# Attention decode with a gMLP branch: load order of x, the third chunk of the last output product, and the shape of two weight pieces

## The chip, the cores and the metric

The kernel runs on one core of a Trainium2 chip. The metric is the device time of one execution in microseconds. A profiled execution also leaves a trace, whose clock starts with the span; all points in time below are microseconds from there.

## The reference

Everything is bf16; B = 4 sequences, one new token each, D = 640.

```python
xn = layernorm(x)
# A: attention over a cache. 32 heads, 4096 keys, head size 128
q = (xn @ wq)                                   # wq: 640 x 4096
p = softmax(q . k_cache * 128**-0.5)            # k_cache, v_cache: 4 x 32 x 4096 x 128
a = (p . v_cache) @ wo                          # wo: 4096 x 640
# B: gated MLP
z = gelu(xn @ w_in)                             # w_in: 640 x 1728, halves z1 and z2
g = w_sp * layernorm(z2) + b_sp                 # w_sp and b_sp are scalars here (one token)
out = x + a + (z1 * g) @ w_out                  # w_out: 864 x 640
```

The two caches are 268 MB of the 282 MB that are read.

## The kernel before

**Loads.** SP's queue carries nearly all bytes, in an order written out in the code: wq (L126), w_in (L129), the first 256 rows of w_out (L132), three pieces of the rest of w_out (`load_piece`, L138), then K and V by units (`load_unit`, L192) and wo (`load_wo`, L200). A unit is 8 heads of one sequence, 8 MB; there are 16 of K and 16 of V. They share five slots of the tile `kv`, so a unit's load waits until what stood in its slot has been read. ACT's queue carries x (L120) and the scalars w_sp and b_sp (L122, L123); POOL's carries two more pieces of w_out (L138) and two small dummy transfers (`step`, L145), which turn POOL's choice of transfer engine so that the pieces fall on chosen ones.

The table `PC` (L62) describes the five pieces: first and last partition, first column chunk, chunks n, and how the rows of w_out are dealt (k, run). Each row of `PC` is one DMA of (last - first) partitions with n / run runs each. The same table drives the z matmuls (L349) and the gelu copies (L363, L366), so that z's columns stand where the rows of w_out do. The pieces land in `w_words`, whose memory the transposed K words take later.

DMAs of SP and ACT take eight completion semaphores in turn, in the order in which the tile framework has placed them; a DMA waits until the one that held its semaphore before has landed. The order before is: w_sp, wq, b_sp, x, w_in, w_out, piece 0, piece 1, piece 2, K unit 0. So piece 2, the ninth, waits for w_sp, and K unit 0 for wq.

**Start.** x waits for a memset on POOL (L118). It goes through a layer norm (L216 to L229) into `xnT` (L233), then q (L304) and z (L342, L349); z runs through gelu, its own layer norm and the gate (L355 to L396), and is multiplied with w_out into `proj` (L409), which frees `w_words`.

**K and V.** DVE transposes K as 32-bit words (L431), PE forms scores (L442); per group of 32 (head, sequence) pairs follow the softmax and the probabilities in `Zb` (L475 to L479). PE multiplies them with V into `O` (L513), and `emit_sel` and `emit_oT` reduce the result to `oT`.

**Tail.** `o_mul` (L556) multiplies a chunk of `oT` with a chunk of wo. The chunks of groups 0 to 2 are summed in `proj`, on partitions 0 to 31 and 32 to 63 by turns, where x (L294) and the gMLP (L409) have been added too. wo of the last group comes in four parts, cut at chunks 4, 6 and 7. Its chunks 0 to 2 still go to `proj`, 320 columns at a time (L604); `o_1` (L608) and `o_q` (L612) then add the two halves of `proj`. Chunks 3 to 7 go to `last`, 160 columns at a time, on two groups of partitions. `o_bf` (L623) adds `last` and `o_q`, and SP and ACT write one half each.

Of the kernel before, what the change touches and what calls it, by code (L numbers as in the profile page):

```python
# [16 lines left out]
def kernel(  # L17
# [19 lines left out]
    nc = tc.nc  # L37
    P = 128
    B, Sq, D = A_x.shape
# [3 lines left out]
    HG = 8  # L43
# [8 lines left out]
    NG = H // HG  # L52
# [6 lines left out]
    nf = FA * P  # L59


    PC = ((0, 20, 0, 10, 5, 10), (32, 44, 0, 11, 3, 11), (0, 4, 10, 3, 3, 1), (60, 68, 0, 24, 2, 24), (92, 96, 0, 18, 3, 6))  # L62
    f_at = [nf]
    for p0, p1, _, n, _, _ in PC:
        f_at.append(f_at[-1] + (p1 - p0) * n)
# [3 lines left out]
    NH = 2  # L69
    NO2 = NOUT // NH  # L70
# [35 lines left out]
    def at_slot(i, n, off=0):  # L106
        return kv[:, i * SL + off:i * SL + off + n]


    x_flat = A_x.rearrange("b s d -> (b s) d")  # L110
# [5 lines left out]
    ln_t = at_slot(0, 8 * D, n_q)  # L116
    XR = 2 * B
    nc.gpsimd.memset(ln_t[:32, :].bitcast(F32).rearrange("p (a n) -> p a n", a=8)[:, 0::7, :], 0.0)  # L118
    x_bf = ln_t[:XR, 0:D]
    nc.scalar.dma_start(out=ln_t[1:XR:2, 0:D], in_=x_flat)  # L120
    sb_bf = const.tile([1, 2], BF16)
    nc.scalar.dma_start(out=sb_bf[:, 0:1], in_=B_w_sp)  # L122
    nc.scalar.dma_start(out=sb_bf[:, 1:2], in_=B_b_sp[None, :])  # L123

    wq = at_slot(0, n_q).rearrange("p (c n) -> p c n", c=DC)
    nc.sync.dma_start(out=wq, in_=A_wq.rearrange("(p c) n -> p c n", c=DC))  # L126
# [9 lines left out]
    def load_piece(eng, t):  # L136
        p0, p1, c0, n, k, run = PC[t]
        return eng.dma_start(out=w_rest[p0:p1, c0:c0 + n].rearrange("p c n -> p (c n)"),  # L138
                             in_=B_w_out[f_at[t]:f_at[t + 1], :].rearrange("(r i c) n -> i r (c n)", i=k, c=run))
# [135 lines left out]
    for q in range(4):  # L275
        nc.gpsimd.tensor_copy(out=SelE[32 * q:32 * q + 32, :, q % 2, :],
                              in_=b8[32 * q:32 * q + 32, 8:8 + HP, None].to_broadcast((32, HP, P // HG)))
# [10 lines left out]
                          in_=ident_f[:].rearrange("p (q x c) -> p q x c", q=2, c=C2))  # L288


    proj = ps_j.tile([64, 512], F32)
# [8 lines left out]
    for hf in range(2):  # L300
        for c in range(DC):
            for j in range(NG):
                n0 = j * HG * Dh + hf * 512
# [21 lines left out]
    z_in = [[], [], [], []]  # L325
    for t, (p0, p1, _, n, k, run) in enumerate(PC):
        src = w_z[:, :, :, f_at[t]:f_at[t + 1]]
        for q in range(p0 // 32, (p1 - 1) // 32 + 1):
            x0, x1 = max(p0, 32 * q), min(p1, 32 * q + 32)
            if x1 - x0 == p1 - p0 and run == n:  # L330
                cols = [src]
            elif run == 1:
                cols = [src.rearrange("p d a (r i) -> p d a i r", i=k)]
            else:
                i_r = src.rearrange("p d a (r i c) -> p d i a r c", i=k, c=run)
                cols = [i_r[:, :, i] for i in range((x0 - p0) * k // (p1 - p0), (x1 - p0) * k // (p1 - p0))]
            z_in[q].append((t, x0 - 32 * q, x1 - 32 * q, cols))
    z_of = [[sum((x1 - x0) * PC[t][3] for t, x0, x1, _ in z[:m]) for m in range(len(z) + 1)] for z in z_in]
    w_za = w_z[:, :, :, 0:nf].rearrange("p c a (q j i) -> p c q a i j", q=4, j=32)
    for c in range(DC):  # L340
        for q in range(4):
            nc.tensor.matmul(z_ps[32 * q:32 * q + 32], lhsT=xnT[:, c, :], rhs=w_za[:, c, q], start=(c == 0), stop=(c == DC - 1))  # L342
        for q in range(4):
            parts = []
            for m, (t, x0, x1, cols) in enumerate(z_in[q]):
                f = (x1 - x0) * PC[t][3] // len(cols)
                parts += [(z_of[q][m] + f * i, f, src) for i, src in enumerate(cols)]
# [8 lines left out]
    for q in range(4):  # L356
        rows = slice(32 * q, 32 * q + 32)
        for m, (t, x0, x1, _) in enumerate(z_in[q]):
            p0, p1, c0, n, k, run = PC[t]
            z = zr_ps[rows, :, z_of[q][m]:z_of[q][m + 1]]  # L360
# [3 lines left out]
            else:  # L364
                for a in range(2):
                    nc.scalar.activation(out=dst[:, a].rearrange("p c (i r) -> p c i r", i=k),  # L366
                                         in_=z[:, a].rearrange("p (r i c) -> p c i r", i=k, c=n), func=ACT.Gelu_apprx_tanh)
# [184 lines left out]
    def o_mul(dst, g, c, hf, n0, n1, start, stop):  # L552

        nb = 32 if start else RW
        c0 = RW * c + 1 - hf
        nc.tensor.matmul(dst[0:nb, 0:n1 - n0], lhsT=state[("oT", g)][:, c0:c0 + nb], rhs=wo_t[g][:, c, n0:n1],  # L556
                         start=start, stop=stop)
# [43 lines left out]
    emit_oT(NG - 1)  # L601
    emit_proj(NG - 2, (1,))

    for c, hf in ((0, 0), (1, 0), (0, 1), (1, 1), (2, 0), (2, 1)):  # L604
        p = min(c, 1)
        o_mul(proj[32 * p:32 * p + 32], NG - 1, c, hf, hf * NO2, (hf + 1) * NO2, False, (c, hf) in ((0, 1), (2, 1)))
    o_1 = ppool.tile([32, NO2], F32, tag="p", name="o_1")
    nc.vector.tensor_copy(out=o_1[:], in_=proj[0:32, 0:NO2])  # L608
    NQ = NO2 // 2
# [2 lines left out]
        nc.vector.tensor_tensor(out=o_q[32 * k:32 * k + 32, :], in0=proj[32:64, k * NQ:(k + 1) * NQ],  # L612
                                in1=o_1[:, k * NQ:(k + 1) * NQ], op=ALU.add)
    last = ps_l.tile([64, NQ], F32)
    for c in range(3, HG):
        for hf in range(NH):
            for k in range(2):
                n0 = hf * NO2 + k * NQ
                o_mul(last[32 * k:32 * k + 32], NG - 1, c, hf, n0, n0 + NQ, c == 3 and hf == 0,
                      c == HG - 1 and hf == NH - 1)  # L620

    o_bf = ppool.tile([64, NQ], BF16, tag="p", name="o_bf")
# [32 lines left out]
```

## Time and profile before

| what | value |
|---|---|
| three runs | 663.15, 663.48, 663.49 us; median 663.48 |
| profiled execution | 663.49 us; span in its trace 661.7 us |
| busy share of the span | DVE 57%, PE 43%, ACT 11%, POOL 11% |
| read from HBM | 282.26 MB, 427 GB/s over the span |
| first load issued | 0.72 us |
| x issued on ACT, its first reader starts | 1.57, 10.94 us |
| first K unit issued | 17.58 us |
| last DVE operation (L623), output issued | 658.89, 659.24 us |

The page's slices cut the span into 40 parts of 16.5 us with each engine's busy share in tenths. The chain of waits goes back from the last instruction, at each step to what released it. In the timeline a row has start, duration, engine, line and operation, and in brackets how long the engine was idle before it and which work ended that. The trace also records single packets of the transfer engines (queue, start, time, size) and the moments at which semaphores count up; a DMA counts up once for each transfer engine that carries a share of it, as that share lands.

### The profile page before, as it was taken

Reading aid. Unit: us, or ns where it says so; the run is one execution under the profiler, and the core shown is the slowest. Engines: PE = TensorE matmul, PEld = TensorE weight load, DVE = VectorE, ACT = ScalarE, POOL = GpSimd, SP = SyncE. Lnnn points to the kernel's source line nnn. Section 1 sums busy time; section 2 is a strip of 40 time slices with the busy share of each in tenths; the row PEclk is TensorE's granted clock in tenths of the full one; section 3 lists DMA queues with packets and bytes.
Section 4 is the critical chain, followed back from the end, with each engine's and each line's share of the span. In section 5 each row is a group of like instructions: output and inputs, shape, how many; then the busy total and the mean of one; then the engine's idle time right before and its main releaser. Section 6 shows DMA issues by size and latency. Waiting matters only on the chain.

```text
span 661.7 us, 5539 instructions
## 1 busy us (share of the span) xinstructions
PE 284.1 (43%) x2303; PEld 108.1 (16%) x2303; DVE 379.7 (57%) x307; ACT 74.1 (11%) x145; POOL 74.2 (11%) x140
## 2 busy tenths in 40 slices
PE   0445555446062356335325065532606254641246
PEld 0221111112021121111102022110202112220012
DVE  6339989766191758718356196764619175971112
ACT  0310000240100000330200000070100000042200
POOL 4540000030200000130300000030110000002300
PEclk9998778679677686766959587765858759666768
DMA  8999999999999999999999999999999999999997
GB/s 367 474 413 428 425 440 445 440 421 428 417 444 441 440 405 436 441 441 440 421 440 412 441 426 439 440 433 424 437 432 440 433 428 415 454 424 437 422 418 288
DMA packets 7241, 282.61 MB, mean 427 GB/s; under 512 B 1120, under 2 KB 1405, under 8 KB 1801
## 3 DMA queue, kind: packets, MB, share of 16 engines
q1 hardware_dynamic: 6837, 281.91, 98.8%
q8 instruction: 18, 0.29, 0.2%
q0 software_dynamic: 352, 0.35, 0.2%
q14 instruction: 6, 0.05, 0.0%
q10 hardware_dynamic: 28, 0.01, 0.0%
HBM read 282.26 MB, written 0.01 MB: 427 GB/s over the span
## 4 chain that ended last, share of the span: by engine, by line
DMA 71%; DVE 12%; issue 11%; PE 2%; POOL 1%; ACT 1%; SPq 0%; DVEq 0%; POOLq 0%; ACTq 0%
DMA kv<-in_A_k_cache_dram 59%; DVE w_words L431 11%; DMA kv<-in_A_v_cache_dram 5%; DMA kv<-in_B_w_in_dram 4%; DMA kv<-in_A_wo_dram 4%; PE O L513 1%; POOL kv L393 0%; PE proj L409 0%; DVE w_words L493 0%; DVE w_words L475 0%; POOL z_b L395 0%; POOL kv L378 0%; ACT L355 0%; DVE m L449 0%; ACT w_words L487 0%
## 5 line engine op out<-in xcount | busy, mean ns | idle before, releaser
L431 DVE STREAM_TRANSPOSE w_words<-kv 128x2048 f32<-128x2048 f32 x128 | 282.8, 2275 | 121.3 <-DMA kv<-in_A_k_cache_dram 118.7
L442 PE MATMUL S<-w_words,QZ 128*32 128x512 bf16 x1024 | 182.7, 488 | 256.1 <-DVE w_words L431 256.1
L442 PEld LDWEIGHTS <-QZ 128*32 128x32 bf16 x1024 | 58.8, 109 | 377.8 <-issue 313.6
L513 PE MATMUL O<-kv,w_words 128*32 128x512 bf16 x1024 | 73.2, 449 | 57.9 <-DMA kv<-in_A_v_cache_dram 50.8
L479 ACT ACTIVATE w_words<-w_words,MkE 32x128 bf16<-32x128 bf16 x120 | 60.9, 507 | 115.8 <-PE O L513 102.7
L522 DVE TENSOR_TENSOR om<-O,Mk 128x512 f32<-128x512 f32 x15 | 10.4, 692 | 94.1 <-PE O L513 94.1
L477 POOL TENSOR_SCALAR w_words<-w_words,MkE 32x128 bf16<-32x128 bf16 x60 | 43.4, 723 | 137.3 <-PE O L513 108.4
L513 PEld LDWEIGHTS <-w_words 128*32 128x32 bf16 x1024 | 33.5, 110 | 96.9 <-issue 67.6
L487 ACT ACTIVATE w_words<-S,negmax 128x1024 bf16<-128x1024 f32 x4 | 4.5, 1114 | 400.1 <-DVE negmax L459 311.7
L475 DVE TENSOR_SCALAR w_words<-w_words,MkE 32x128 bf16<-32x128 bf16 x76 | 24.6, 324 | 2.3
L417 POOL COPY QZ<-qT 32x32 bf16<-32x32 bf16 x16 | 5.1, 318 | 173.0 <-PE S L442 172.5
L523 DVE TENSOR_REDUCE R<-om 128x128 f32<-128x512 f32 x15 | 15.3, 1020 | 0.5
L498 POOL TENSOR_SCALAR rs<-MkB,rowsum 128x4 f32<-128x4 f32 x4 | 1.2, 299 | 112.7 <-ACT w_words L487 112.7
L493 DVE STREAM_TRANSPOSE w_words<-w_words 128x1024 bf16<-128x1024 bf16 (+1 forms) x8 | 9.6, 1241 | 5.6 <-ACT w_words L487 5.6
L546 POOL MEMSET oT<- 128x66 bf16 x4 | 0.5, 156 | 97.5 <-PE proj L556 97.5
L449 DVE TENSOR_REDUCE m<-S 128x1 f32<-128x1024 f32 x4 | 4.9, 1225 | 6.1 <-PE S L442 6.1
L133 DVE MEMSET w_words<- 128x7680 f32 x1 | 6.5, 6458 | 2.4 <-issue 2.4
L535 PE MATMUL misc<-R,SelX 128*128 128x512 f32 x8 | 4.5, 645 | 7.2 <-DVE R L523 5.5
L525 DVE TENSOR_SCALAR R<-O,Mk 128x128 f32<-128x128 f32 x1 | 0.4, 351 | 12.5 <-PE O L513 12.5
L304 PE MATMUL q<-kv,xnT 128*32 128x512 bf16 x40 | 4.5, 631 | 6.5 <-DVE xnT L233 6.5
L500 PE MATMUL misc<-rs,SelE 128*128 128x4 f32 x8 | 2.3, 364 | 10.4 <-POOL rs L498 10.4
L556 PE MATMUL proj<-kv,oT 128*8 128x320 bf16 x54 | 5.2, 333 | 1.6 <-DMA kv<-in_A_wo_dram 1.6
(105 smaller groups left out, 95.1 us busy)
## 6 DMA issues: line engine op xcount, KB each, us to landing
kv<-in_A_k_cache_dram SPq DMA_DIRECT2D x8, 4096.0 KB, 30.1
kv<-in_A_v_cache_dram SPq DMA_DIRECT2D x1, 6144.0 KB
kv<-in_A_wq_dram SPq DMA_DIRECT2D x1, 5120.0 KB, 16.8
kv<-in_A_wo_dram SPq DMA_DIRECT2D x3, 1280.0 KB
kv<-in_B_w_in_dram SPq DMA_DIRECT2D x1, 2160.0 KB, 23.9
kv<-in_A_v_cache_dram SPq DMA_DIRECT2D x1, 2048.0 KB
kv<-in_A_wo_dram SPq DMA_DIRECT2D x1, 640.0 KB, 23.6
kv<-in_B_w_out_dram SPq DMA_DIRECT2D x1, 320.0 KB
```

The costliest lines, as they stand in the source:

```text
L133: nc.vector.memset(w_words[:, 0:FR * NOUT // 2], 0.0)
L417: nc.gpsimd.tensor_copy(out=QZ[r0:r0 + 32, :, :, :, 8 + 8 * hp], in_=qT[32 * g:32 * g + 32, NE * hp:NE * hp + NE].rearrange("p e a b -> p ...
L431: nc.vector.transpose(kT.rearrange("p (t r) -> p t r", r=32), kw)
L442: nc.tensor.matmul(S_ps[32 * q:32 * q + 32, i], lhsT=QZ[:, b, 2 * kh + w, e, w0:w0 + 32], rhs=kb[:, i, :, e, :, w], start=(b == 0 and k < ...
L475: nc.vector.tensor_scalar(out=dst, in0=src, scalar1=mk, scalar2=None, op0=ALU.mult)
L477: nc.gpsimd.tensor_scalar(out=dst, in0=src, scalar1=mk, scalar2=None, op0=ALU.mult)
L479: nc.scalar.activation(out=dst, in_=src, func=ACT.Copy, scale=mk)
L493: nc.vector.transpose(pT_t[:, j0:j1, :], blocks)
L513: nc.tensor.matmul(O_ps[32 * q:32 * q + 32, :, :], lhsT=Zb[b % 2][:, w].rearrange("p h c -> p (h c)"), rhs=vv[:, w * 4 * Dh:(w + 1) * 4 * ...
L522: nc.vector.tensor_tensor(out=om4[:], in0=O_ps[:], in1=Mk4[:, :, None].to_broadcast((P, 4, Dh)), op=ALU.mult)
L523: nc.vector.tensor_reduce(out=R, in_=om4[:].rearrange("p c d -> p d c"), axis=AX.X, op=ALU.add)
L556: nc.tensor.matmul(dst[0:nb, 0:n1 - n0], lhsT=state[("oT", g)][:, c0:c0 + nb], rhs=wo_t[g][:, c, n0:n1], start=start, stop=stop)
```

## The change

It has three parts. x is loaded as two DMAs of two rows each on ACT's queue, and the two scalars are held back until the second of them has been issued. Two pieces of w_out, piece 2 on SP and piece 4 on POOL, go on three partitions instead of four, with the same number of rows and half as many runs; the special case of a run of one goes. In the tail, chunk 2 of the last group moves from `proj` to `last`. Since the number of DMAs ahead of the K loads grows by one and x now comes behind wq in the count, the waits on the eight semaphores move too: the order is wq, x part one, x part two, w_sp, b_sp, w_in, w_out, piece 0, piece 1, piece 2, K unit 0.

```diff
-    PC = ((0, 20, 0, 10, 5, 10), (32, 44, 0, 11, 3, 11), (0, 4, 10, 3, 3, 1), (60, 68, 0, 24, 2, 24), (92, 96, 0, 18, 3, 6))
+    PC = ((0, 20, 0, 10, 5, 10), (32, 44, 0, 11, 3, 11), (0, 3, 10, 4, 2, 2), (60, 68, 0, 24, 2, 24), (92, 95, 0, 24, 2, 12))
...
-    nc.scalar.dma_start(out=ln_t[1:XR:2, 0:D], in_=x_flat)
+    for b0 in range(0, B, 2):
+        x_in = nc.scalar.dma_start(out=ln_t[1 + 2 * b0:5 + 2 * b0:2, 0:D], in_=x_flat[b0:b0 + 2, :])
     sb_bf = const.tile([1, 2], BF16)
-    nc.scalar.dma_start(out=sb_bf[:, 0:1], in_=B_w_sp)
-    nc.scalar.dma_start(out=sb_bf[:, 1:2], in_=B_b_sp[None, :])
+    with tc.issue_after(x_in.ins):
+        nc.scalar.dma_start(out=sb_bf[:, 0:1], in_=B_w_sp)
+        nc.scalar.dma_start(out=sb_bf[:, 1:2], in_=B_b_sp[None, :])
...
-            elif run == 1:
-                cols = [src.rearrange("p d a (r i) -> p d a i r", i=k)]
...
-    for c, hf in ((0, 0), (1, 0), (0, 1), (1, 1), (2, 0), (2, 1)):
-        p = min(c, 1)
-        o_mul(proj[32 * p:32 * p + 32], NG - 1, c, hf, hf * NO2, (hf + 1) * NO2, False, (c, hf) in ((0, 1), (2, 1)))
+    for c, hf in ((0, 0), (1, 0), (0, 1), (1, 1)):
+        o_mul(proj[32 * c:32 * c + 32], NG - 1, c, hf, hf * NO2, (hf + 1) * NO2, False, hf == NH - 1)
...
-    for c in range(3, HG):
+    for c in range(2, HG):
         for hf in range(NH):
             for k in range(2):
                 n0 = hf * NO2 + k * NQ
-                o_mul(last[32 * k:32 * k + 32], NG - 1, c, hf, n0, n0 + NQ, c == 3 and hf == 0,
+                o_mul(last[32 * k:32 * k + 32], NG - 1, c, hf, n0, n0 + NQ, c == 2 and hf == 0,
                       c == HG - 1 and hf == NH - 1)
```

## The prediction

> **What bounds the kernel now.** I read the page first: the slices (part 2), the queues (part 3) and the chain (part 4).
>
> ```profile
> span 661.7 us, 5539 instructions
> DMA  8999999999999999999999999999999999999997
> q1 hardware_dynamic: 6837, 281.91, 98.8%
> q8 instruction: 18, 0.29, 0.2%
> DMA 71%; DVE 12%; issue 11%; PE 2%; POOL 1%; ACT 1%; SPq 0%; DVEq 0%; POOLq 0%; ACTq 0%
> ```
>
> The transfer engines are busy from the first slice to the last: queue 1, which SP feeds, alone takes 98.8% of sixteen engines' span. The chain's "DMA 71%" understates this; its DVE and issue parts lie beside running transfers, since each load is issued while earlier ones are still queued. The load of K unit 2 shows how far ahead: issued at 54.88, while the engine that is first through K unit 1 lands its part only at 59.84 (semaphore records of the trace). So a delay in the first 50 us costs nothing unless it leaves an engine's ring empty.
>
> Next the chain of waits over the last 22 us.
>
> ```profile
> 633.20 23.64 DMA kv<-in_A_wo_dram
> 656.84 0.04 issue
> 656.88 0.44 PE proj L556 x4
> 657.32 0.06 PE last L556
> 657.38 0.22 PE proj L556 x2
> 657.60 0.02 issue
> 657.63 0.49 DVE o L608
> 658.12 0.02 issue
> 658.14 0.32 DVE o_q L612
> 658.46 0.01 issue
> 658.47 0.33 DVE o_q L612
> 658.80 0.03 issue
> 658.83 0.02 DVEq L623
> 658.85 0.04 issue
> 658.89 0.32 DVE o_bf L623
> ```
>
> It names DVE as last before `o_bf`, but by a hair: PE's last matmul into `last` ends at 658.76, as the last piece of wo lands at 658.41.
>
> Third, the timeline of the start.
>
> ```profile
> 1.57 0.68 ACTq L120 DMA_DIRECT2D kv<-in_A_x_dram  x1
> 8.88 2.49 SPq L138 DMA_DIRECT2D w_words<-in_B_w_out_dram  x3
> 18.16 4.46 PE L304 MATMUL q<-kv,xnT 128*32 128x512 bf16 x40 [6.54 <-DVE xnT L233]
> 25.08 0.30 PE L342 MATMUL misc<-kv,xnT 128*32 128x128 bf16 x4 [2.46 <-DMA kv<-in_B_w_in_dram]
> ```
>
> x feeds the layer norm, then q; but what PE waits for next, 2.46 us long, is w_in, not x.
>
> **The tail.** Two 320-column matmuls of chunk 2 leave `proj`; four of 160 columns join `last`. `proj` is then complete with the group of four that ends at 657.32 (individual records: 657.32 for the last of them) rather than at 657.59, so `o_1` and both `o_q` move 0.27 us forward and end at about 658.53. Now PE is last: its end at 658.76 stays, since the four matmuls of chunk 7 start only when that chunk has landed (658.41), and PE has gaps ahead of chunks 4, 6 and 7. From PE's end to DVE's start took 0.04 us at L608 (657.59 to 657.63). So `o_bf` starts at 658.80 instead of 658.89: **-0.10 us**, all that this edit can give; 0.17 of the 0.27 us meet the wait for the last piece. The extra two matmuls (about 0.07 us each at the pitch of `last`, 1.33 us for 18) lie in the gap before chunk 4, which lands at 657.61. Were that cover gone they would cost up to 0.14 us.
>
> **x ahead, in two parts.** Before, the semaphore records show three rows of x landing at 8.94 to 9.19 and the fourth at 10.90, on the engine that had carried both scalars, the second of which landed at 7.83. On that engine packets of ACT's queue take turns with packets of wq: the second scalar's word at 5.83, its semaphore at 7.39, the row of x at 8.91, each one wq packet (1.51 us) apart. After, part one waits for POOL's memset (ends 1.34) and is issued at about 1.4, part two at about 2.0. Each engine used carries a row and a semaphore, and where both parts use the same engines that twice over: four turns, the first at 5.8 to 7.0, the last 4.54 us later, plus 0.5 to land: 10.8 to 12.0. If the parts went to different engines, 8.9 to 9.2. I take the first, since two scalars from ACT shared one engine.
> The Trainium skill (DMA: Bandwidth & Descriptors, the section on why a DMA increments its semaphore by 16) says that a DMA runs on the lowest-numbered k engines, k dividing the slowest dimensions. By that both parts sit on engines 0 and 1, which speaks against the split; the trace agrees, with x and the scalars meeting on one engine.
> Either way it costs nothing: q would end at 22.62 + 1.1 = 23.7 at the latest, before w_in lands at 25.04. Beyond that, z's chain has 4.96 us of queued loads as cover (59.84 - 54.88). The scalars, now behind x, land before 20 and are used at 29.03.
>
> **Pieces on three partitions.** The same rows in half as many descriptors. SP's piece 2: 12 packets of 1,280 B at 0.055 us become 6 of 2,560 B at 0.102: 0.66 to 0.61 us on its one engine. POOL's piece 4: 12 of 7,680 B at 0.291 (3.49 us) become 6 of 15,360 B, between 0.291 and 0.615 (16,384 B) and near the latter; by interpolation 0.575, 3.45 us. PE's z matmuls stay at 40 of L349 and ACT's gelu at the same elements. The engine that got x's fourth row carries one more row of x (+0.055). All this is under 0.1 us on single engines, and none is the last one: at the landing of 658.41 the last engine trails the next by 0.15 us, and it became last in one step of 1.5 us at 634.9, where the 17th instruction packet (16,384 B on queue 8, 1.10 us) fell on it. Effect 0 (between -0.04 and +0.06).
>
> **The moved waits.** Of the DMAs of SP and ACT each takes the next of eight semaphores and waits until its last holder has landed. One more DMA, and x behind wq in the count, shift the holders. Piece 1 now waits for wq (17.56) where it waited for nothing; piece 2 for part one of x; K unit 0, which waited for wq, for part two of x. Queued behind piece 1 on SP are piece 2 and K unit 0, and K unit 0's issue moves from 17.58 to 17.58 + 0.75 + 0.69 (the issues of pieces 1 and 2) + 0.09 = 19.11. Eight engines have no pieces of queue 1; the packet records show seven of them reaching K unit 0 at 20.73 to 20.98 and the eighth at 21.37. From issue to first packet there is one row with empty rings, wq: issued 0.72, first packets 1.75 to 2.77, that is 1.03 to 2.05 later. Counted until it streams at full rate (first packet of 1.51 us done at 3.97 to 4.88) it is 1.74 to 2.65. So K unit 0 can start at 20.14 to 21.16, or stream from 20.85 to 21.76. Seven engines may lose 0 to 1.03 us, the eighth 0 to 0.39. The eighth, by its distance to the others, is the one that ends last (2.9 us ahead at 45.55, and last after two steps of 1.5 us, each at an instruction packet), so it counts in full. The other seven have cover: 0.31 us for one of them, which the 18th fetch hits, and 1.8 or more for the rest. A gain is excluded, since a later issue brings nothing forward. Cost: **0 to +0.72 us** (1.03 - 0.31); I take +0.1, since wq's start was cold and here all queues run.
> The Trainium skill (the same page, on latency) gives 0.6 us to a first byte from SP's queue; by that the rings would never run dry and the term is 0. Wq's row of 1.03 and more differs, and I go by the row.
>
> **Sum.** The profiled execution took 663.49 us, 1.79 more than its span, and stands 0.01 over the median of the three runs (663.48). 663.49 - 0.10 (tail) + 0 (x) + 0 (pieces) + 0.1 (K unit 0) = **663.5**. A measurement of this kernel tells some 0.2% (1.3 us) from no change.
>
> **Rivals.**
> *The ring runs dry (slower).* K unit 0 comes so late that the last engine stalls. For it: 1.53 us later on SP, with 1.6 us from the new issue to the first empty ring. Against: the last engine has 2.26 us (21.37 - 19.11), and only its loss counts. Each microsecond after that is one at the end, so it is over 0.2% from 3.7 us between issue and stream (2.26 + 1.33 + 0.10), 1.0 more than wq's worst. It would give about 665.0. A late part two of x does the same, from 17.56 + 1.5 = 19.1 on. Chance 0.14.
> *The engines end more evenly (faster).* At 658.41 the sixteen engines lead the last one by 0 to 2.48 us, 1.09 on average. Perfect balance would give 663.49 - 1.09 - 0.10 = 662.3, still within 0.2%, but nothing here moves bytes between the last engine and the others. Over 0.2% needs more than balance: 0.04.
> *x is on the path (faster or not as said).* If x set the start, part one at 9.0 instead of 10.9 would give -1.9 us, 661.6. Against it stands the 2.46 us wait for w_in. Chance 0.01.
> *The main case*, all covers hold: 0.81, with 663.39 to 664.1 by the bounds above.
>
> **Numbers.** Median noise adds 0.3 us on either side. The range from 662.8 to 664.9 leaves out the dry ring's long end and the small gains. Faster by over 0.2% 0.05, within 0.2% 0.81, slower 0.14.
>
> **What would show it.** In the profile after: `o_bf` waits for PE's `last`, not `o_q`, and starts some 0.04 us after PE's end; the first K issue of L194 on SP stands near 19.1 with pieces 1 and 2 between 17.6 and 19.1; slices of DMA still 9; PE's wait before the z matmuls still ends on w_in near 25. Wrong would be: a DMA slice of 8 near 20 us, last wo landing later than 658.9 or earlier than 658, or z's matmuls waiting for q or x.

## The result and the profile after

The changed kernel takes 664.37 us (median of 22 runs, 664.00 to 664.71) against 663.35 for the kernel before on the same chip (22 runs, 663.15 to 663.53): +1.02 us, a ratio of 1.0016 [1.0009, 1.0022]. That is a small, real loss, just inside the 0.2% that the prediction set as the bound of no change, and 0.9 us above its number. The profiled execution took 664.16 us, with a span of 662.2.

The page after: span, slices (busy share of the transfer engines in tenths, and GB/s, per 1/40 of the span) and chain.

```profile
span 662.2 us, 5547 instructions
...
DMA  9999999999999999999999999999999999999997
GB/s 369 435 428 431 425 424 452 435 428 431 433 439 432 443 399 449 440 440 431 409 435 432 439 420 444 431 432 424 441 439 443 428 428 413 435 440 443 421 412 290
...
DMA 74%; issue 10%; DVE 9%; PE 4%; POOL 1%; ACT 1%; SPq 0%; DVEq 0%; POOLq 0%; ACTq 0%
```

And the GB/s line of the page of before, which the prediction had not shown:

```profile
GB/s 367 474 413 428 425 440 445 440 421 428 417 444 441 440 405 436 441 441 440 421 440 412 441 426 439 440 433 424 437 432 440 433 428 415 454 424 437 422 418 288
```

The busy line says 9 from end to end, but the second slice (16.6 to 33.1 us) shows 435 GB/s where it showed 474. The line counts a packet whole in the slice in which it starts, which makes the fall look larger than it is: with each packet spread over its own time, the slice moves 408 GB/s where it moved 429. By the packet records, spread in this way, 34.27 MB had moved by 82.7 us after the change and 34.59 before; at 427 GB/s the 0.32 MB are 0.75 us, and the gap is there by 30 us (11.45 and 11.79 MB). Some 0.25 us of it are engines without a packet (the time in packets between 20 and 25 us, averaged over the sixteen engines, falls from 5.07 to 4.83 us; the records overlap a little); the rest are packets that take longer. A longer packet counts as busy, and 0.25 us is little in a slice of 16.5, so the sign that the prediction named (a busy slice of 8) could not show this.

The timeline of SP, and then of PE, at the start:

```profile
8.88 10.36 SPq L140 DMA_DIRECT2D w_words<-in_B_w_out_dram  x3
19.28 0.38 SPq L194 DMA_DIRECT2D kv<-in_A_k_cache_dram  x1
```

```profile
19.26 3.88 PE L306 MATMUL q<-kv,xnT 128*32 128x512 bf16 x40 [6.34 <-DVE xnT L235]
25.56 0.24 PE L342 MATMUL misc<-kv,xnT 128*32 128x128 bf16 x4 [2.42 <-DMA kv<-in_B_w_in_dram]
```

The three pieces, which took SP's queue 2.49 us, now stretch over 10.36: piece 1 is issued at 17.77, piece 2 at 18.56 (the single instructions in the trace), K unit 0 at 19.28 instead of 17.58. q starts 1.1 us later and z's matmuls still wait for w_in (landed at 25.52, before at 25.04), so x is not on the path.

The chain at the end:

```profile
634.96 24.17 DMA kv<-in_A_wo_dram
659.13 0.04 issue
659.17 0.32 PE last L556 x4
659.49 0.02 issue
659.51 0.32 DVE o_bf L622
```

PE is now last before `o_bf`, as the tail edit intends (`o_q` had ended at 659.24). But the last piece of wo lands at 659.13, and landed at 658.41 before: +0.72 us, and all that follows comes that much later, less the 0.10 of the tail (`o_bf` 659.51 against 658.89).

### The profile page after: what moved, and what is told of

Read it like the earlier page. It is cut to its first block, busy times and chain, and to the rows that moved or that the text cites. A ratio compares the mean times of both kernels' runs of the same rounds, so it can differ in the third digit from the quotient of the medians.

```text
span 662.2 us, 5547 instructions
## 1 busy us (share of the span) xinstructions
PE 290.1 (44%) x2305; PEld 109.1 (16%) x2305; DVE 379.6 (57%) x307; ACT 74.1 (11%) x145; POOL 73.0 (11%) x140
## 4 chain that ended last, share of the span: by engine, by line
DMA 74%; issue 10%; DVE 9%; PE 4%; POOL 1%; ACT 1%; SPq 0%; DVEq 0%; POOLq 0%; ACTq 0%
DMA kv<-in_A_k_cache_dram 46%; DMA kv<-in_A_v_cache_dram 21%; DVE w_words L431 9%; DMA kv<-in_B_w_in_dram 4%; DMA kv<-in_A_wo_dram 4%; PE O L513 3%; POOL kv L393 0%; PE proj L409 0%; POOL z_b L395 0%; PE S L442 0%; SPq L202 0%; POOL kv L378 0%; ACT L355 0%; PE misc L342 0%; DVE z_b L396 0%
## 5 line engine op out<-in xcount | busy, mean ns | idle before, releaser
L442 PE MATMUL S<-w_words,QZ 128*32 128x512 bf16 x1024 | 188.5, 501 | 252.2 <-DVE w_words L431 252.2
L513 PE MATMUL O<-kv,w_words 128*32 128x512 bf16 x1024 | 75.6, 460 | 56.0 <-DMA kv<-in_A_v_cache_dram 52.8
```

Source lines behind the costliest of these rows:

```text
L442: nc.tensor.matmul(S_ps[32 * q:32 * q + 32, i], lhsT=QZ[:, b, 2 * kh + w, e, w0:w0 + 32], rhs=kb[:, i, :, e, :, w], start=(b == 0 and k < ...
L513: nc.tensor.matmul(O_ps[32 * q:32 * q + 32, :, :], lhsT=Zb[b % 2][:, w].rearrange("p h c -> p (h c)"), rhs=vv[:, w * 4 * Dh:(w + 1) * 4 * ...
```

## The experiments

A transfer engine works through what is queued for it, its ring; the ring runs dry when the engine has finished that before the next load arrives.

**Theory:** K unit 0 is issued too late to reach the transfer engines before eight of them run out of queued work. The transfer engines have no idle time later in which to make that up, so the loss stays to the end. **Rivals:** the pieces or the tail cost it; the two parts of x cost it; more DMAs cost it as such; the pieces issued late right in front of K unit 0 do.

All results first. "First packets" are the first 64 KB packets of K unit 0 on the eight engines without pieces: the range of their starts and of the time each took. An undisturbed one takes 2.42 us; one that takes longer is called stretched. "Moved" is what all packets had carried by 82.7 us. The change of the median is against the kernel before on the same chip.

| kernel | K unit 0 issued | first packets start | took | moved, MB | last wo landed | median |
|---|---|---|---|---|---|---|
| before | 17.58 | 20.73–21.37 | 2.42 | 34.59 | 658.41 | |
| x one part, scalars late (e9) | 11.40 | 20.37–21.02 | 2.42 | 34.61 | 658.20 | +0.01 |
| pieces only (e2) | 17.72 | 20.54–21.03 | 2.42 | 34.64 | 658.01 | +0.06 |
| tail only (e3) | 17.78 | 20.52–21.05 | 2.42 | 34.60 | 658.20 | -0.06 |
| scalars late (e4) | 17.80 | 20.44–21.02 | 2.42–2.48 | 34.62 | 658.09 | +0.12 |
| K unit 0 behind a DVE copy (e10) | 17.82 | 20.61–21.10 | 2.42–2.47 | 34.62 | 658.20 | +0.04 |
| x one part (e7) | 18.34 | 20.63–22.42 | 2.78–4.13 | 34.28 | 659.51 | +1.30 |
| one spare load (e5) | 18.41 | 20.86–22.08 | 2.64–3.79 | 34.24 | 659.71 | +1.29 |
| K unit 0 behind DVE transposes (e12) | 18.78 | 20.92–21.73 | 2.81–3.72 | 34.22 | 660.07 | +1.39 |
| two spare loads (e6) | 19.18 | 20.87–21.68 | 2.83–3.46 | 34.27 | 659.08 | +1.46 |
| x part only (e1) | 19.24 | 20.74–22.04 | 2.51–3.72 | 34.24 | 659.14 | +1.37 |
| **the change** | 19.28 | 20.80–21.87 | 2.74–3.57 | 34.27 | 659.13 | +1.02 |
| K unit 0 behind a POOL copy (e11) | 19.54 | 21.13–22.14 | 2.53–3.56 | 34.22 | 659.36 | +1.26 |
| three spare loads (e8) | 20.16 | 21.50–22.67 | 2.62–3.89 | 34.06 | 660.02 | +2.31 |

**The three parts, one at a time.** The kernel before with the x part alone, the new `PC` alone, and the new tail alone (the diffs are those of the change).

> Only the x part of the change on the kernel before: two parts of x ahead of the scalars, so that the waits move as in the whole change. Theory (K unit 0 issued 1.7 us later, rings of eight transfer engines run empty near 20.8 us): first K issue at 19.2 to 19.4, last piece of wo lands 0.5 to 0.8 us later than before, time +0.9 to +1.2 us. Rival A (the new piece shapes slow single engines): 0. Rival B (later x delays the z chain): also slower, but then PE's wait before the z matmuls no longer ends on w_in.

> Only the three-partition pieces. Theory: within 0.15 us of before, first K issue at 17.6. Rival A: +0.7 to +1.0 us.

> Only chunk 2 moved to last. Theory: -0.10 us, PE's last ends the wait of o_bf, which starts 0.02 to 0.05 us after PE's end. A rival in which the two extra matmuls are in the way: 0 to +0.14 us.

x alone: 664.57 against 663.20, 1.0020 [1.0012, 1.0029]. Pieces alone: 663.26, 1.0001 [0.9992, 1.0010]. Tail alone: 663.14, 0.9999 [0.9991, 1.0008]. The loss sits in the x part. At +1.37 us that part alone costs more than I had expected (+0.9 to +1.2), and 0.35 more than the whole change; no run takes this difference apart. The tail's 0.1 us is smaller than the runs can resolve; its mechanism shows in the chain of the tail alone, where PE takes DVE's place and `o_bf` follows it at once:

```profile
658.20 0.04 issue
658.25 0.32 PE last L556 x4
658.57 0.02 issue
658.59 0.32 DVE o_bf L622
```

**x's two parts or K unit 0.** The whole change, with the scalars issued later still, behind the activation of rstd. x keeps its two parts and lands as late, but K unit 0 again waits for wq, as before, and no piece waits.

```diff
-    with tc.issue_after(x_in.ins):
-        nc.scalar.dma_start(out=sb_bf[:, 0:1], in_=B_w_sp)
-        nc.scalar.dma_start(out=sb_bf[:, 1:2], in_=B_b_sp[None, :])
...
+    act = nc.scalar.activation(out=rstd[:], ...)
+    with tc.issue_after(act.ins):
+        (the two scalars)
```

> The whole change, but the two scalars are loaded after the first square root on ACT, behind K unit 0 in the count of semaphores: piece 1 and piece 2 wait for nothing, K unit 0 waits for wq as before. x stays in two parts and lands as late as in the change. Theory: first K issue back at 17.6, no stretched first packets, time -0.1 us against before (663.25). Rival A or B: still +0.9 to +1.1 us.

663.32 against 663.20, 1.0002 [0.9993, 1.0011]: the loss is gone. SP's timeline and the GB/s line of this run:

```profile
8.88 2.48 SPq L137 DMA_DIRECT2D w_words<-in_B_w_out_dram  x3
17.80 0.36 SPq L191 DMA_DIRECT2D kv<-in_A_k_cache_dram  x1
```

```profile
GB/s 370 471 413 428 425 439 447 436 421 424 430 440 441 440 403 438 441 441 432 429 424 428 441 418 443 440 425 436 438 432 428 429 436 419 446 436 422 423 425 296
```

The pieces are back in one group, K unit 0 is 1.48 us earlier, and the second slice is 471 again. x in two parts costs nothing, nor do more DMAs as such, since this run has as many as the change; where they stand in the count of semaphores does.

**The same with x in one part.** K unit 0 then is eighth and waits for no semaphore.

> The whole change, but x in one DMA ahead of the scalars, and the scalars behind the first square root on ACT: now K unit 0 is the eighth DMA in the count and waits for nothing, so it is issued at about 11.4 instead of 17.6. Theory: no ring was empty before, so this gains nothing over the version with late scalars; with the tail's 0.1 us 663.1 to 663.3. Rival (even at 17.6 the issue of K unit 0 costs something): 662.8 or less.

Issued at 11.40, six microseconds earlier than before, for 663.26 against 663.25, 1.0000 [0.9991, 1.0009]. Earlier than needed brings nothing.

**Spare loads: a dose of lateness.** The kernel before with one, two or three more loads of w_sp on ACT into a scratch tile, which shift the semaphores like the change does.

```diff
+    spare = const.tile([1, 2], BF16)     # [1, 4] for three
+    for i in range(1):     # 2, 3
+        nc.scalar.dma_start(out=spare[:, i:i + 1], in_=B_w_sp)
```

> The kernel before with one more DMA on ACT behind x: a second load of the scalar w_sp into a spare tile that nobody reads. It moves the count of semaphores by one: piece 2 waits for wq, K unit 0 is issued behind it. Nothing else of the change is in it. Theory: K unit 0 issued at 18.4 to 18.5; with the 2.6 us from issue to full rate that the change showed it streams from 21.1, where the first rings end at 20.5 to 20.9: 0.2 to 0.6 us lost on the early engines, most of it covered at the end; time +0.1 to +0.4 us. Rival (x's place or its two parts, not the waits, made the change slow): 0.

> The kernel before with two such spare loads on ACT: pieces 1 and 2 and K unit 0 are all issued behind wq, as in the change; x, pieces and tail as before. Theory: K unit 0 issued at 19.2, time +1.0 to +1.4 us, as the x part alone gave. Rival: 0.

> Three such spare loads: piece 0 waits for wq as well, so K unit 0 is issued at about 20.2, one microsecond later than with two. Theory: rings empty from 20.5 on for all engines, each further microsecond of delay is one at the end: +1.8 to +2.4 us. Rival (a fixed loss for any gap): as with two.

One: 664.54 against 663.25, 1.0020 [1.0011, 1.0029]. Two: 664.71, 1.0022 [1.0013, 1.0031], at +1.46 just above what I had expected. Three: 665.56, 1.0034 [1.0022, 1.0047]. Here my expectation of one load failed: I had it at +0.1 to +0.4 by adding a fixed delay to the issue, and it cost as much as two. So the medians make no ramp: nothing up to 17.82, then at once 1.3, flat to 19.3, and 2.3 at 20.16. With three loads, though, piece 0 is late too (17.64 instead of 8.88), so that last step is not K unit 0's lateness alone. And single runs spread at the edge: with one load ten of eleven runs lie between 664.48 and 664.94, and one at 663.56.

**x in one part, whole change otherwise.** Fewer DMAs, K unit 0 half as late.

```diff
-    for b0 in range(0, B, 2):
-        x_in = nc.scalar.dma_start(out=ln_t[1 + 2 * b0:5 + 2 * b0:2, 0:D], in_=x_flat[b0:b0 + 2, :])
+    x_in = nc.scalar.dma_start(out=ln_t[1:XR:2, 0:D], in_=x_flat)
```

> The whole change, but x in one DMA, still ahead of the two scalars. As many DMAs as before; x in the first place shifts the completion semaphores, so piece 2 waits for wq near 17.6 us and K unit 0 queues behind it, issued near 18.4 us instead of 19.28. The tail and the pieces on three partitions stay. Theory one (any issue later than about 17.8 us empties the rings): +0.9 to +1.4 us, 664.1 to 664.6. Rival (the second part of x is what costs): 0 to +0.2 us, 663.2 to 663.4.

664.55 against 663.25, 1.0018 [1.0009, 1.0026]. The second part of x is not what costs. Its eleven runs spread from 663.56 to 664.96, and three of them lost only 0.3 to 0.8 us.

**K unit 0 alone late.** In all late cases so far a piece was issued late too, right in front of K unit 0. In these three the kernel before keeps its pieces at 9.9 and 10.7 us, and K unit 0 waits for a small write into its slot (with the GpSimd copy, a memset that GpSimd ran at 19.60 goes behind it, to 20.42):

```diff
-    load_unit(seq[0])
...
+    nc.vector.tensor_copy(out=at_slot(3, 1)[96:128], in_=xnT[96:128, 0, 0:1])            # e10, behind xnT
+    k_gate = nc.gpsimd.tensor_copy(out=at_slot(3, 1)[96:128], in_=SelN[96:128, 1, 0:1])  # e11, behind SelN
+    for j in range(2):                                                                   # e12, behind xnT
+        nc.vector.transpose(at_slot(3, DC * 32)[96:128].rearrange("p (c j) -> p c j", c=DC), xn_v[:, 3])
+    load_unit(seq[0])
```

> The kernel before, with one tiny VectorE copy into K unit 0's slot right behind the transposes of xnT; K unit 0 is overwritten on it and so must wait for it. No DMA is added: pieces 1 and 2 stay at 9.9 and 10.7 us, and K unit 0 alone goes from 17.58 to about 18.4 us, as late as in the run with one more load, where two pieces were issued right in front of it. Theory one (K unit 0's own lateness empties the rings, and the restart is slow): +1.0 to +1.4 us, 664.2 to 664.6, K unit 0's first packets stretched past 2.6 us, last wo landing near 659.2. Rival (the late pieces in front of K unit 0 do it, or add to it): +0.1 to +0.4 us, 663.4 to 663.6, first packets at most 2.6 us.

> The same, with the tiny copy on GpSimd behind the four steps of SelN that end at 19.05 us: K unit 0 alone goes to about 19.3 us, as late as in the change, with pieces 1 and 2 at 9.9 and 10.7. Theory one (K unit 0's own lateness): +1.0 to +1.5 us, 664.2 to 664.8, last wo landing near 659.1; a plain delay line, where each later microsecond of issue costs one, would put it 0.9 us above the run with the VectorE copy. Rival (the late pieces do it): +0.2 to +0.6 us.

> The kernel before, with two spare VectorE transposes (0.35 us each) into K unit 0's slot right behind the four of xnT, and K unit 0 waiting for them: K unit 0 alone goes from 17.58 to about 18.4 us, with pieces 1 and 2 at 9.9 and 10.7. At 17.82 (the tiny VectorE copy, which came sooner than meant) nothing was lost; at 19.54 alone (the GpSimd copy) 1.26 us. Theory one (a step at about 18 us, then flat): +1.0 to +1.4 us, 664.2 to 664.7, first packets of K unit 0 stretched past 2.6 us. Rival (alone, the loss grows with the delay from about 18 us on, and at 18.4 the piece right in front made it what it was): +0.2 to +0.6 us, 663.5 to 663.9.

The VectorE copy came sooner than I had placed it, so K unit 0 left at 17.82 and this run tests another dose than meant: 663.29 against 663.25, 1.0002 [0.9993, 1.0011]. It marks the edge. Ten of its eleven runs lie between 663.12 and 663.35, and one at 664.33; that the rings ran dry in that one is likely but not shown, since only one execution is profiled. The GpSimd copy: 664.51 against 663.25, 1.0020 [1.0011, 1.0029], with the pieces early, as SP's timeline shows:

```profile
8.88 2.49 SPq L138 DMA_DIRECT2D w_words<-in_B_w_out_dram  x3
19.54 0.36 SPq L192 DMA_DIRECT2D kv<-in_A_k_cache_dram  x1
```

The transposes, at 18.78 instead of the 18.4 that I had worked out: 664.68 against 663.29, 1.0020 [1.0011, 1.0029]. SP's timeline and the GB/s line of this run:

```profile
8.88 2.49 SPq L138 DMA_DIRECT2D w_words<-in_B_w_out_dram  x3
18.78 0.36 SPq L192 DMA_DIRECT2D kv<-in_A_k_cache_dram  x1
```

```profile
GB/s 370 429 435 431 422 433 440 435 428 439 428 439 436 435 412 439 436 436 443 440 407 431 436 425 440 449 428 423 428 431 439 440 439 408 451 432 419 437 416 264
```

The three pieces leave as in the kernel before (2.49 us together), K unit 0 alone is 1.2 us later, and the second slice falls to 429. So K unit 0's lateness by itself is enough, and the late pieces are not needed. Both expectations of "theory one" held (+1.26, +1.39). Between 17.82 and 18.78 no run has K unit 0 late alone; the doses of 18.34 and 18.41 have one late piece in front of it.

No version ran measurably faster than the kernel before; the lowest, the tail alone, is 0.06 us below it, inside its interval.

## Why the prediction was right or wrong

**Right in range and kind, too low in its number.** The time, 664.37, lies within 662.8 to 664.9 and within 0.2% of before. It lies 0.27 us above the main case's own bounds (663.39 to 664.1) and 0.6 below the dry ring's 665.0. What the rings did was the rival's mechanism at a lower price; the main case's sentence that all covers hold was wrong. That the time still fell into the range is luck: the range reached 0.8 us beyond the main case's bounds, for noise and for a part of the rival.

**The term that was mis-sized is K unit 0.** I took +0.1 out of 0 to +0.72. The last landing moved by +0.72 in the profiled execution. That this is my upper bound is an accident: I had 1.03 less the cover of 0.31 of another engine, and gave the one that ends last at most 0.39. The medians want about 1.1 (1.02 and the 0.10 that the tail gives back), and the x part alone +1.37. Three readings behind it failed:

- *From issue to full rate.* I took wq's cold start as the longer one: 1.74 to 2.65 us, and argued that running queues would be quicker. Here the first packets ended at 24.30 to 24.60; less their undisturbed 2.42 us, they stand for a start at 21.88 to 22.18, that is 2.6 to 2.9 us after the issue at 19.28. Here the running queues were the slower. By this, an estimate, K unit 0 had to be issued by about 18.0 (20.73 - 2.7) to lose nothing; the runs found the edge between 17.82 and 18.34. The kernel before then had some 0.4 us to spare, and the change is 1.3 us past the edge, although 1.6 us seemed left "from the new issue to the first empty ring". The 2.6 to 2.9 us are no fixed lead: read in the same way, the runs with issues from 18.34 to 18.78 needed 2.8 to 4.6.
- *Who loses.* The first packets, which had ended between 23.14 and 23.79, now ended between 24.30 and 24.60: the median engine lost 1.16 us, where I gave at most 1.03, and the last of the eight, which I gave 0 to 0.39, lost 0.81.
- *The form.* "Each microsecond after that is one at the end" is not so near the edge: in the medians, a miss of 0.3 us (18.34) cost as much as one of 1.5 (19.54).

The Trainium skill (DMA: Bandwidth & Descriptors, "Latency and other measured facts") gives 0.6 us to a first byte. By that the rings would never have run dry; the runs decide against it as a lead. Counted from the end of the issuing instruction instead of its start, it does fit the quickest engine at the cold start (wq: 1.12 to 1.75, 0.63 us), but the slowest took 1.65 us there, and with three spare loads the first packets of K unit 0 came 0.94 to 2.11 us after the end of its issue (20.56). The same section gives up to 2 us for an HBM access at high load. An estimate from both figures, 2.6, is near the 2.6 to 2.9 of the change, but not near the 2.8 to 4.6 closer to the edge; no run separates the two.

**What held.** Where the waits go: piece 1 waits for wq, piece 2 and K unit 0 queue behind it, and K unit 0 is issued at 19.28 (19.11 worked out, since a piece in that place takes as long and part two of x was in time). x: landed at 12.04 to 12.09 where 10.8 to 12.0 was worked out, first read at 12.22 instead of 10.94, and free, as the run with late scalars shows. The pieces: packets of 15,360 B took 0.573 us (0.575 in the prediction; its two rows interpolate to 0.577), those of 2,560 B 0.102, effect none. The tail: `o_bf` waits for PE and starts 0.04 us after the last matmul's end in the trace (659.48 to 659.51). z waits for w_in. And of the signs named as wrong, one came: last wo later than 658.9.

**The engine that ends last.** As before, it is the eighth of those without pieces, on which the first, ninth and seventeenth instruction packets fall: after the seventeenth (635.63, 1.10 us on queue 8) it trails the next by 0.53 us. The eighteenth brings a second one level with it (659.12 and 659.13 at the end). So of the 1.16 us that the median engine lost in the first 25 us, the engine that decides paid what it had lost itself, 0.72 to 0.81.

## What to carry to other kernels

Where the transfer engines set the time, find the first load whose queue position depends on a wait, and compare its issue with the moment at which the engines reach it. Here an issue 2.9 us ahead (17.82 for 20.73) lost nothing, one 2.4 us ahead (18.34) lost 1.3, and nothing later gave it back. A small DMA added or moved anywhere ahead can shift every wait behind it when completion semaphores are taken in turn: list who waits for whom before and after, not only who moved. And read GB/s, not the busy share, to see a queue run dry: the busy share stayed at 9. For the size of the loss go to the packets, since the GB/s of a slice counts those that start in it.

## What the runs showed of the hardware

**A ring that ran dry cost about 1.2 us at once.** Issued at 18.34 to 19.54, K unit 0 cost 1.0 to 1.5 us in the medians, with no slope, and 2.31 at 20.16, where piece 0 was late too. In those runs its first 64 KB packets do not start later by as much; they are stretched, from 2.42 to between 2.5 and 4.1 us.

**Others are stretched with them.** In the run with the transposes, where the pieces had been queued since 10.7 us, packets of w_in (17,280 B) between 22 and 24 us took up to 1.11 us instead of 0.64, and those of piece 1 (14,080 B) up to 0.99 instead of 0.53, on engines that had not yet come to K unit 0. So the restart slowed other engines too for some 2 us, which would make the loss a step. The cold start of the kernel before looks alike: wq's first packets of 40,960 B took 1.64 to 2.56 us, later ones of that size 1.51 to 1.54. What it is that the engines share, and why it costs about the same for 0.3 us of lateness as for 1.5, stays open; no run here takes it apart.

**Instruction packets cost transfer time.** Eighteen packets of 16,384 B on queue 8 took 0.96 to 1.12 us each, before and after the change. By the landings of the loads they fall in turn on the eight engines without pieces, and they decide which engine is last.
